# Six of nine chunks multiplied in pairs by one level of Strassen's scheme, with weight sums streamed from DRAM

## The chip, the core and the metric

The kernel runs on one core of a Trainium2 chip. TensorE multiplies, VectorE (DVE), ScalarE (ACT) and GpSimd (POOL) do elementwise work, SyncE (SP) issues DMAs. The metric is device time in microseconds: 858.1 as the median of three runs (858.06 to 858.86). The profile is one further execution, whose span is 856.1 us.

## The reference

Linear attention for 8 batches of 8 heads, 576 tokens of width 64, and an MLP behind it:

```python
q_s = softmax(q, axis=-1); k_s = softmax(k, axis=2)      # both with 1e-9 in the denominator
kv = np.einsum('bhsd,bhse->bhde', k_s, v)
x  = np.einsum('bhsd,bhde->bhse', q_s, kv)               # to 4608 tokens x 512
h  = x @ w_in                                            # 512 -> 2048
g  = h * np.tanh(softplus(h))
out = g @ w_out                                          # 2048 -> 512
```

Everything is fp32. The two products with w_in and w_out are nearly all of the arithmetic.

## The kernel before

**Precision.** TensorE takes operands in a rounded fp32 form (F32R). To keep fp32 accuracy each operand is split into a high part and a low part, the rounded value and what is left, and every product is made of three matmuls: high x high, high x low, low x high. A split costs a rounding copy (the high part) and a subtraction (the low part). The weights come in as 64-bit integers that hold a double; lines 123 to 177 turn them into such pairs on ScalarE, VectorE and GpSimd during the first 115 us.

**Chunks and slots.** Each batch gives a chunk of 512 tokens (its first 512); the 64 remaining tokens of all batches make the ninth chunk, collected through a DRAM tile, `xt_dram`. A chunk has 16 slots, one per block of 128 hidden columns. A slot multiplies first: `h_part` (line 527) adds 4 blocks of 128 input rows x 3 matmuls of 128x512 into one PSUM bank, `ph`. Then Mish on ScalarE (`g_mish`, 553), the high part on VectorE (`g_hi`, 558) and the low part (`g_lo`, 563). Three slots later (`LAG`) `out_mm` (569) adds 4 token blocks x 3 matmuls of 128x512 into four PSUM banks, `po`. So a slot is 12 + 12 matmuls of 128x512, and a chunk 192 + 192.

**Attention items.** 32 items (a batch and two heads each) run beside the MLP: maxima, sums and transposes on VectorE, exponentials on ScalarE (which change its function table, and Mish changes it back), the subtraction of the maximum and the multiplication with the reciprocal on GpSimd (`a_qsub` 270, `a_qmul` 369). Two items make a pair, whose small matmuls `a_pair` (469) places between two blocks; it ends with the split of the chunk's input rows (`x_hi` 509, `x_lo` 514).

**Order.** Everything is scheduled by hand: each engine runs its instructions in the order in which the program issues them. The head of the program is a list of tokens, `FIRST` (line 22): each names a function and its arguments, and a dictionary, `stages`, maps names to functions. It covers the conversion of the weights, the first 8 items and chunk 0 up to its output block 12. From there `group` (601) is a loop: four slots and one attention item per turn, the same for every chunk. DMAs are issued by SP in that same order.

**Memory.** SBUF holds the split weights for the whole run: two tiles `wi` (high and low, 4 x 2048 columns each) and sixteen tiles `wo`. The inputs of two chunks lie in buffers `xa` and `xb`.

Of the kernel before, what the change touches and what calls it, by code (L numbers as in the profile page):

```python
# [43 lines left out]

FILL = dict(
# [8 lines left out]
def attn_mish_mlp(ctx: ExitStack, tc: tile.TileContext, q, v, k2, v2, wu, qs, kt, out):  # L54
# [14 lines left out]
    NSLOT = (B + 1) * NF  # L69
# [10 lines left out]
    sp = ctx.enter_context(tc.tile_pool(name="sp", bufs=4))  # L80
# [11 lines left out]
    turn = []  # L92

    def turn_bank(name):
        turn.append("gh"["gh".index(turn[-1]) ^ 1] if turn else "g")
        return bank(turn[-1], name)


# [7 lines left out]
    wi = [cp.tile([P, HP, DFF], F32R, tag=f"wi{x}", name=f"wi{x}") for x in "hl"]  # L106
# [7 lines left out]

    conv = {}
# [7 lines left out]
    def w_load(j):  # L123
        kind, f = units[j]
        st = xp.tile([P, SM, 2], U32, tag=STAGED.split()[j], name=f"raw_{kind}{f}")
        nc.sync.dma_start(st, wu[f + (NF if kind == "out" else 0)].bitcast(U32).rearrange("p (c z) -> p c z", z=2))
        conv[j] = [st[:, :, 0], st[:, :, 1]]
# [28 lines left out]
    def w_dst(j):  # L156
        kind, f = units[j]
        a = conv[j][2].bitcast(F32)
        if kind == "out" and f not in wo:
            wo[f] = xp.tile([P, 2, DM], F32R, tag=f"wo{f}", name=f"wo{f}")  # L160
        if kind == "in":
            return a.rearrange("p (t c) -> p t c", t=HP), [w[:, :, f * P:(f + 1) * P] for w in wi]
        return a, [wo[f][:, 0], wo[f][:, 1]]
# [20 lines left out]
    xt_dram = dp.tile([B, P, HP, ST], F32, name="xt_dram")  # L184
# [144 lines left out]
    def a_ksub2(f, s):  # L329
        if f >= NITEM:  # L330
            return
        k2, mb = at[f]["k"][:, parts[s]], at[f]["mb"].rearrange("p (h d) -> p h d", h=2)
        sub(nc.vector, k2, k2, mb.unsqueeze(1).to_broadcast(list(k2.shape)))
# [39 lines left out]
    def a_qt(i, b=None):  # L373
# [3 lines left out]
        if i >= COLS:  # L377
            qe = r["qe"].rearrange("p n f -> p (n f)")
            if i % 2:
                qT, qTt = sp.tile([P, SM], F32, tag="wc", name=f"qT{i}"), ap_odd[:, 0]  # L380
# [14 lines left out]
    def a_qt2(i):  # L395
        r = at[i]
        if i in (0, 2, 5, 7):

            t = lp.tile([P, S], F32, tag="kt", name=f"qT{i}") if i < HP else xp.tile([P, S], F32, tag="xb3", name=f"qT{i}")
# [69 lines left out]
    def a_pair(e):  # L469


        f = e + 2
        px = [bank("ef"[j], f"px{e + j}") for j in range(2)] if e >= COLS else None
        if px:
            a_x2(e, px, None, [(0, j, h) for j in range(2) for h in range(2)])
        r = [turn_bank(f"pt{e}_{j}") for j in range(2)]
        pkv = [r[j][:, ST:ST + D + 2] for j in range(2)]
        if px:
            a_x2(e, None, [t[:, 0:ST] for t in r], [(1, j, h) for j in range(2) for h in range(2)])
        if f < NITEM:  # L480
            a_kv2(f, pkv)
        if px:
            for j in range(2):
                x_hi(e + j, at[e + j]["px"])
                x_lo(e + j, at[e + j]["px"])
            for j in range(2):
                a_tail2(e + j)
                a_tail3(e + j)
        if f < NITEM:
            a_kvs2(f)  # L490


# [12 lines left out]
    def a_tail3(i):  # L505
        b, hp = divmod(i, HP)
        nc.sync.dma_start(xt_dram[b, :, hp, :], at[i]["xt"])

    def x_hi(i, src):
        b, hp = divmod(i, HP)  # L510
        xs[i] = xp.tile([P, 2, SM], F32R, tag=f"x{'ab'[b % 2]}{hp}", name=f"xs{i}")
# [4 lines left out]

    tails = {}

    def t_load(t):
        x = tails[t] = pools["wp"].tile([P, SM], F32, tag="w", name=f"xtl{t}")  # L520
        nc.sync.dma_start(x.rearrange("p (b s) -> p b s", b=B), xt_dram[:, :, t, :].rearrange("b p s -> p b s"))

# [4 lines left out]
    def h_part(n, t, b=None):  # L527
        c, f = divmod(n, NF)
        if t == 0:
            gs[n] = bank(b, f"ph{n}") if b else turn_bank(f"ph{n}")  # L530
            fill(f"H{n}", gs[n])
        fs = slice(f * P, (f + 1) * P)
        x = xs[c * HP + t]
        for i, (a, z) in enumerate(((0, 0), (0, 1), (1, 0))):
            nc.tensor.matmul(gs[n], wi[a][:, t, fs], x[:, z], start=t == 0 and i == 0,  # L535
                             stop=t == HP - 1 and i == 2)

    def h_mm(n):
        for t in range(HP):
            h_part(n, t)  # L540

    def open_pools():
        ap.tile([P, 36], F32, tag="gap", name="gap")
        start.__exit__(None, None, None)
        pools["wp"] = ctx.enter_context(tc.tile_pool(name="wp", bufs=4))
        pools["rp"] = ctx.enter_context(tc.tile_pool(name="rp", bufs=LAG + 1))
# [22 lines left out]
    def out_mm(n, parts=range(NC)):  # L569
        c, f = divmod(n, NF)  # L570
        if f == 0:
            for t in range(NC):
# [4 lines left out]
    def out_part(n, t):  # L577
        f = n % NF

        end = NF - 1 - LAG if n // NF == B and t == NC - 1 else NF - 1  # L580
        out_cols(po[t], n, t, slice(0, DM), f == 0, f == end)

    def out_cols(dst, n, t, e, first, last):
        f, g = n % NF, gs[n]
        for i, (a, z) in enumerate(((0, 0), (0, 1), (1, 0))):
            nc.tensor.matmul(dst, g[a][:, t * P:(t + 1) * P], wo[f][:, z, e], start=first and i == 0,  # L586
                             stop=last and i == 2)

    def evac(c, t, copy, cols=slice(0, DM)):
        ob = sp.tile([P, DM], F32, tag="wc", name=f"ob{c}_{t}")[:, cols]  # L590
        copy(ob, po[t])  # L591
        if c < COLS // HP:
            nc.sync.dma_start(out[c * S:c * S + SM, :].rearrange("(p c) e -> p c e", c=NC)[:, t, :], ob)
        elif c < B:
            nc.sync.dma_start(out[c * S + t * P:c * S + (t + 1) * P, :], ob)
        else:
            for j, eng in enumerate((nc.sync, nc.scalar)):
                e = (2 * t + j + 1) * S
                eng.dma_start(out[e - ST:e, cols], ob[j * ST:(j + 1) * ST])

    def group(n):
        i = HP + n // G

        f = i + 1 if i % 2 else i + 2
        pair = i - 1 if i % 2 and COLS < i < NITEM else COLS - 2 if i == COLS else None
        for u in range(G):
            m, o = n + u, n + u - LAG
            if m < NSLOT:
                h_mm(m)
            split = u == 2 and pair is not None  # L610
            if split:
                g_mish(m)
                if pair < COLS:
                    out_mm(o, (0, 1))
                a_pair(pair)
            if u == 0:
                if NITEM <= i < NITEM + HP:
                    t_load(i - NITEM)
                a_qsum(i)
                if i < NITEM:  # L620
                    a_qmul(i)
            if u == 1:
                a_qt(i)
                if i == COLS:
                    a_ksub2(i, 0)
                    a_ksub2(i, 1)
                elif i % 2:
                    a_ksub2(f, 1)
            if 0 <= o < NSLOT:
                out_mm(o, (2, 3) if split and pair < COLS else range(NC))  # L630
            if m < NSLOT and not split:
                g_mish(m)
            if 0 <= o < NSLOT and o % NF == NF - 1:
                for t in range(NC):
                    evac(o // NF, t, nc.scalar.copy if t % 2 else nc.vector.tensor_copy)
            if m < NSLOT:
                g_hi(m)
                g_lo(m)
            if i == COLS and u < 3:
                a_kmx(i + 1 + u)  # L640
                kt_load(i + 3 + u)
            elif i % 2 == 0 and u in (0, 2):
                a_kmx(f + u // 2)
                kt_load(f + u // 2 + 2)
            if u == 1:
                if i == COLS:
                    a_exp2(i, 0)
                    a_exp2(i, 1)
                elif i % 2:
                    a_exp2(f, 1)  # L650
                if pair is not None:

                    nc.scalar.activation(early, ident[:, 0:1], AF.Mish)
                a_qm(i + 1)
            if u == 2:
                if pair is not None:
                    k_load(pair + 4)
                    v_load(pair + 4)
                elif NITEM <= i < NITEM + HP:
                    x_hi(i, tails[i - NITEM])  # L660
                    x_lo(i, tails[i - NITEM])
            if u == 3 and i % 2 == 0:
                a_ksub2(f, 0)
        if i % 2 == 0:
            a_exp2(f, 0)
        a_exp(i + 1)
        q_load(i + 2)
# [15 lines left out]
        G=g_hi, GA=lambda n: g_hi(n, act.copy), GL=g_lo, O=out_mm)  # L683
    with tc.manual_schedule(engines={ET.Activation, ET.PE, ET.DVE, ET.Pool, ET.SP}):
        for token in first:
            name, number, banks = re.fullmatch("([A-Z]+)([0-9]*)([a-h]*)", token).groups()
            stages[name](*([int(number)] if number else []), *([banks] if banks else []))
            if name == "H" and banks in ("g", "h"):
                turn[:] = [banks]
        for n in range(NF, NSLOT, G):  # L690
            group(n)


        end = range(NSLOT - LAG, NSLOT)
        base = sp.tile([P, DM], F32, tag="wc", name="base")
# [68 lines left out]
```

## Time and profile before

| | before |
|---|---|
| median of 3 runs | 858.1 us |
| profiled execution, span | 856.1 us |
| PE busy | 846.2 us (99%) |
| PEld busy | 690.4 us (81%) |
| DVE busy | 433.3 us (51%) |
| ACT busy | 322.8 us (38%) |
| POOL busy | 127.9 us (15%) |
| DMA | 66.39 MB, mean 78 GB/s |

PE is TensorE's matmuls, PEld its weight loads. Matmuls are pipelined and overlap in the records, so that their single durations (about 390 ns) add up to more than the busy time; the pace is read from the starts of blocks. The chain of waits is followed back from the last instruction, at each step to what released it. A row of the windows view gives, for one stretch of the span, the busy microseconds of PE, PEld, DVE, ACT and POOL with their instruction counts, then the granted TensorE clock, the busy share of the 16 DMA engines, and GB/s. A row of the groups view ends with the number of instructions, busy time and mean duration in ns, and the idle time before them with its releaser.

### The profile page before, as it was taken

To read this page: it belongs to the slowest core of one execution; us is meant where nothing else is said; L and a number is where in the kernel's file an instruction comes from. 1 tells how busy PE (TensorE), PEld (TensorE's weight loads), DVE (VectorE), ACT (ScalarE), POOL (GpSimd) and SP (SyncE) were. 2 spreads that over 40 slices of the span, in tenths; PEclk is the share of its full clock that TensorE was granted. 3 is DMA by queue.
4 is the path that set the end of the run, shared out by engine and by line. 5 is a ranking of instruction groups with operands and counts; after the bars stand their busy time and mean duration, and the time that the engine had idled before them with its cause. 6 is when DMAs were issued, how large, how long until landed. Compare 5 with 4: busy or idle time off the path is not lost.

```text
span 856.1 us, 12563 instructions
## 1 busy us (share of the span) xinstructions
PE 846.2 (99%) x4951; PEld 690.4 (81%) x4951; DVE 433.3 (51%) x1111; ACT 322.8 (38%) x498; POOL 127.9 (15%) x111
## 2 busy tenths in 40 slices
PE   8999999999999999999999999999999999999998
PEld 7677778888888888888888888888887888888886
DVE  7998775554645455455545465546543222222221
ACT  6998644424342435243432434243423121111111
POOL 6897110110011111110111110111110000000000
PEclk9999999999999999999999999999999999999999
DMA  9984134212221121212221222121000020001001
GB/s 342 392 322 138 40 115 148 74 42 74 80 72 42 56 85 41 85 29 87 77 81 35 74 91 73 30 74 64 18 14 2 15 75 13 1 1 50 0 1 50
DMA packets 32667, 66.39 MB, mean 78 GB/s; under 512 B 11488, under 2 KB 11744, under 8 KB 32608
## 3 DMA queue, kind: packets, MB, share of 16 engines
q1 hardware_dynamic: 32208, 65.06, 22.9%
q8 instruction: 39, 0.64, 0.3%
q10 hardware_dynamic: 400, 0.52, 0.2%
q14 instruction: 20, 0.16, 0.1%
HBM read 55.09 MB, written 10.49 MB: 77 GB/s over the span
## 4 chain that ended last, share of the span: by engine, by line
PE 90%; DMA 4%; DVE 3%; ACT 1%; issue 1%; SPq 1%; POOL 0%; DVEq 0%
PE po L586 44%; PE ph L535 42%; PE px L414 2%; DMA raw_out<-in_w_dram 2%; DMA v<-in_v_dram 2%; PE pt L451 2%; DMA k<-in_k_dram 1%; DVE wa L148 1%; DVE wc_out L154 1%; DVE k L113 0%; DVE wc_in L154 0%; DVE gl L113 0%; PE po_last L586 0%; PE pt L414 0%; SPq L209 0%
## 5 line engine op out<-in xcount | busy, mean ns | idle before, releaser
L535 PE MATMUL ph<-xs,wih 128*128 128x512 f32 x1152 | 356.4, 391 | 1.3 <-ACT qT L406 1.0
L586 PE MATMUL po<-wo,gh 128*128 128x512 f32 x1146 | 354.8, 391 | 0.0
L535 PEld LDWEIGHTS ph<-xs,wih 128*128 128x128 f32 x1152 | 214.8, 188 | 48.7 <-ACT qT L406 1.4
L586 PEld LDWEIGHTS po<-wo,gh 128*128 128x128 f32 x1146 | 214.0, 188 | 46.0 <-issue 0.8
L555 ACT ACTIVATE y<-ph 128x512 f32<-128x512 f32 x128 | 76.7, 599 | 412.4 <-PE ph L535 345.6
L535 PE MATMUL ph<-xs,wil 128*128 128x512 f32 x576 | 224.3, 389 | 0.0
L586 PE MATMUL po<-wo,gl 128*128 128x512 f32 x573 | 223.1, 389 | 0.0
L560 DVE CAST gh<-y 128x512 fp32r<-128x512 f32 x128 | 54.6, 426 | 266.2 <-ACT y L555 266.1
L535 PEld LDWEIGHTS ph<-xs,wil 128*128 128x128 f32 x576 | 108.1, 188 | 22.6
L586 PEld LDWEIGHTS po<-wo,gl 128*128 128x128 f32 x573 | 107.5, 188 | 22.6
L113 DVE TENSOR_TENSOR gl<-y,gh 128x512 fp32r<-128x512 f32 x128 | 89.4, 699 | 11.9
L371 POOL TENSOR_TENSOR qe<-qe,qs 128x576 f32<-128x576 f32 x24 | 27.9, 1161 | 304.2 <-DVE qs L367 304.2
L113 POOL TENSOR_TENSOR q<-q,qm 128x576 f32<-128x576 f32 (+1 forms) x32 | 38.0, 1192 | 204.9 <-DVE qm L256 194.7
L555 ACT ACT_TABLE_LOAD x24 | 30.8, 1283 | 49.0 <-PE ph L535 48.9
L515 DVE TENSOR_TENSOR xs<-px,xs 128x512 fp32r<-128x512 f32 x32 | 20.6, 686 | 42.9 <-ACT xs L512 42.9
L339 ACT ACT_TABLE_LOAD x23 | 29.5, 1283 | 5.5 <-DVE k L113 5.1
L357 DVE TENSOR_REDUCE qs<-qe 128x18 f32<-128x576 f32 x24 | 18.1, 752 | 25.8 <-ACT qe L346 25.8
L265 DVE TENSOR_REDUCE qm<-q 128x18 f32<-128x576 f32 (+1 forms) x32 | 24.4, 763 | 9.2 <-DMA q<-in_q_dram 4.7
L591 DVE COPY ob<-po 128x512 f32<-128x512 f32 x16 | 11.0, 691 | 26.1 <-PE po L586 26.1
L237 DVE TENSOR_REDUCE mxd<-kt 128x1 f32<-128x576 f32 x32 | 23.8, 745 | 0.5 <-DMA kt<-in_kt_dram 0.5
L246 DVE STREAM_TRANSPOSE mb<-mxd 32x32 f32<-32x32 f32 x96 | 19.4, 202 | 1.8
L113 POOL TENSOR_TENSOR wil<-wc_in,wih 128x512 fp32r<-128x512 f32 x15 | 19.4, 1305 | 5.6 <-ACT wih L167 5.2
(113 smaller groups left out, 563.0 us busy)
## 6 DMA issues: line engine op xcount, KB each, us to landing
kt<-in_kt_dram SPq DMA_DIRECT2D x32, 288.0 KB, 3.0
v<-in_v_dram SPq DMA_DIRECT2D x14, 594.0 KB, 5.5
raw_in<-in_w_dram SPq DMA_DIRECT2D x16, 512.0 KB, 7.7
raw_out<-in_w_dram SPq DMA_DIRECT2D x16, 512.0 KB, 6.7
out_dram<-ob SPq DMA_DIRECT2D x32, 256.0 KB, 2.2
k<-in_k_dram SPq DMA_DIRECT2D x14, 576.0 KB, 4.1
q<-in_qs_dram SPq DMA_DIRECT2D x24, 288.0 KB, 2.8
q<-in_q_dram SPq DMA_DIRECT2D x8, 320.0 KB, 6.2
```

Source lines behind the costliest of these rows:

```text
L113: eng.tensor_tensor(out, a, b, ALU.subtract)
L237: nc.vector.tensor_reduce(mxd, r["kt"], axis=AX.X, op=ALU.max, negate=i < HP)
L246: nc.vector.transpose(mb[o:o + 32, h], mxd[h].to_broadcast([32, 32]))
L265: nc.vector.tensor_reduce(qm, qt, axis=AX.X, op=ALU.max)
L339: nc.scalar.activation(k2, k2, AF.Exp)
L357: nc.vector.tensor_reduce(z, q2, axis=AX.X, op=ALU.add)
L371: eng.tensor_tensor(q2, q2, z.unsqueeze(2).to_broadcast(list(q2.shape)), ALU.mult)
L515: nc.vector.tensor_tensor(xs[i][:, 1], src, xs[i][:, 0].bitcast(F32), ALU.subtract)
L535: nc.tensor.matmul(gs[n], wi[a][:, t, fs], x[:, z], start=t == 0 and i == 0, stop=t == HP - 1 and i == 2)
L555: nc.scalar.activation(y, gs[n], AF.Mish)
L560: copy(hi, gs[n])
L586: nc.tensor.matmul(dst, g[a][:, t * P:(t + 1) * P], wo[f][:, z, e], start=first and i == 0, stop=last and i == 2)
```

## The change

The first three chunks stay as they were. The last six (five batches and the chunk of remaining tokens) are taken in three pairs, k = 0 to 2, and both products of a pair are done by one level of Strassen's scheme in Winograd's form. For the first product the weights are cut in two along the hidden columns and along the 512 input rows (blocks A11, A12, A21, A22) and the inputs along the input rows and along the tokens (B11 ... B22; a token half holds 256 tokens of each of the two chunks). Seven block products take the place of eight:

```
S1 = A21+A22  S2 = S1-A11  S3 = A11-A21  S4 = A12-S2       (weights)
T1 = B12-B11  T2 = B22-T1  T3 = B22-B12  T4 = B21-T2       (inputs)
P1 = A11 B11  P2 = A12 B21  P3 = S4 B22  P4 = A22 T4
P5 = S1 T1    P6 = S2 T2    P7 = S3 T3
C11 = P1+P2   C12 = P1+P6+P5+P3   C21 = P1+P6+P7+P4   C22 = P1+P6+P5+P7
```

(T4, and so P4, is held with its sign such that it adds.) The second product does the same with the Mish values as B and w_out as A, and gives the output transposed, in a second output tensor that the host transposes back.

- **Weight sums.** During chunks 1 and 2, for each of 16 units (8 of w_in, 8 of w_out): GpSimd adds high and low part back together (`w_whole`, 2 additions of 128x512) and forms the four sums (`w_mix`, 4 of 128x256); ScalarE rounds (`w_mix_hi`, 128x1024), VectorE subtracts (`w_mix_lo`, 128x1024), SP stores to a DRAM tile `ws` (`w_keep`, 3 DMAs of the unmixed blocks; `w_mix_out`, 8 DMAs). Together 112 block operands of 256 KB, in the order in which TensorE wants them.
- **Weight stream.** GpSimd fetches two operands at a time (512 KB) into a ring of six SBUF tiles (`w_fetch`), 56 per pair, in the order of the tokens `F0` to `F171`. A fetch waits until TensorE is done with the tile that it overwrites. The tiles are former weight and input buffers.
- **Inputs.** `x_raw` copies the attention result to SBUF unsplit; VectorE forms the four sums (`x_mix`, 128x1024), then each of seven operands is split (`x_mix_hi` on ScalarE, `x_mix_lo` on VectorE, 128x1024).
- **First product.** 8 blocks n x 7 products x 6 matmuls of 128x512. P1, P6, P5, P3 add into one PSUM bank, P7 and P4 into another, P2 into a third. Between them ScalarE copies the partial sum out (`partial`, 24 per pair) and VectorE adds the other bank (`joined`, 24 per pair), and Mish runs on the result (`g_mish_quad`, 32 per pair).
- **Second product.** The Mish values are mixed (`g_mix`, 16 of 128x1024 per pair, alternately VectorE and GpSimd) and split (`g_mix_hi` on ScalarE and `g_mix_lo` on VectorE, 28 each, 128x1024, in a ring of four tiles). Again 56 x 6 matmuls of 128x512. 6 partial copies, 8 joins, 8 stores of 256 KB per pair.
- **Order.** `FIRST` is as before. In place of the loop `group` stands a second list of tokens, `LATER`, for all engines and the whole rest. The attention items run on through chunks 1 and 2 and pair 0, the last ones at the start of pair 1; the items of pair k+1 come during pair k.

```diff
+LATER = """
+WW0 WM0 WK0 HM16g WK1 MK9 WH0 WK2 OP13.0 WK4 WL0 OP13.1 LK11 OP13.2 WK6 YM16 U8.0v OP13.3 WP0 G16 HM17h GL16 U8.1v Q8
...
+GX1.0.1v XR28 A1.3.2 F72 C1.3.0 A1.2.5 J1.3.0 N1.3.0 A1.3.7 C1.2.3 F73 GH1.1.1 J1.2.3 A1.3.6 N1.2.3 GK1.1.1 PK28df
...
+A2.2.7 C2.1.3 J2.1.3 A2.2.6 F126 N2.1.3 A2.1.3 C2.2.2 A2.1.4 N2.1.1 F127 GX2.0.0p A2.3.1 J2.1.2 N2.1.2 A2.3.2 C2.3.0
...
-    wi = [cp.tile([P, HP, DFF], F32R, tag=f"wi{x}", name=f"wi{x}") for x in "hl"]
+    wi = [cp.tile([P, 2, HP, P], F32R, tag=f"w{f}", name=f"wi{f}") for f in range(NF)]
...
+    NW = 14 * NH
+    ws = dp.tile([NW // 2, P, 2, 2 * 2 * P], F32, name="ws")
...
+    def w_whole(j, eng="p"):
...
+            engines[eng].tensor_tensor(a[:, i], w[:, 0].bitcast(F32), w[:, 1].bitcast(F32), ALU.add)
...
+    def x_mix(k, o, eng="v"):
+        b11, b12, b21, b22 = (x_quad(k, kh, th) for kh in range(2) for th in range(2))
+        d, a, b = ((b11, b12, b11), (b12, b22, b12), (b22, b22, b11), (b21, b21, b22))[o]
+        sub(engines[eng], d, a, b)
...
+    RING = ["w0", "w1", "xa0", "xa1", "xa2", "xa3"]
...
+    def w_fetch(e):
+        t = ring[e] = (cp if RING[e % 6][0] == "w" else xp).tile(
+            [P, 2, 2, 2, P], F32R, tag=RING[e % 6], name=f"ws{e}")
+        nc.gpsimd.dma_start(t.rearrange("p s z j c -> p s (z j c)"), ws[e % (NW // 2)].bitcast(F32R))
...
+    def first_product(k, n, p):
+        t = k * NW + place[1, p, n]
+        w = ring[t // 2][:, t % 2]
+        if p in (1, 2, 7):
+            letter = {1: "gac"[n % 3], 2: "h", 7: "eb"[n % 2]}[p]
+            psb[p, k, n] = bank(letter, f"{ {1: 'px', 2: 'pz', 7: 'py'}[p] }{k}_{n}")
+        dst = psb[{6: 1, 5: 1, 3: 1, 4: 7}.get(p, p), k, n]
+        for j in range(2):
+            for i, (a, z) in enumerate(halves3):
+                nc.tensor.matmul(dst, w[:, a, j], xc[k, p][z][:, j].rearrange("p b s -> p (b s)"),
+                                 start=p in (1, 2, 7) and j == 0 and i == 0, stop=j == 1 and i == 2,
+                                 skip_group_check=p not in (1, 2, 7))
...
+    def partial(k, n, q):
+        nc.scalar.copy(g_quad(k, n)[q], psb[1, k, n])
+
+    def joined(k, n, q):
+        g = g_quad(k, n)[q]
+        nc.vector.tensor_tensor(g, psb[2 if q == 0 else 7, k, n], g, ALU.add)
...
+    def g_mix_hi(k, p, h):
+        t = split[k, p, h] = pools["sc"].tile([P, 2, 2, SM], F32R, tag=f"s{ring_at[p, h] % 4}", name=f"gs{k}_{p}_{h}")
+        nc.scalar.copy(t[:, 0], gq[k, h][G_PART[p]])
+
+    def g_mix_lo(k, p, h):
+        t = split[k, p, h]
+        sub(nc.vector, t[:, 1], gq[k, h][G_PART[p]], t[:, 0].bitcast(F32))
...
-        for n in range(NF, NSLOT, G):
-            group(n)
...
+        for token in first + LATER.split():
+            name, numbers, letters = re.fullmatch("([A-Z]+)([0-9.]*)([a-z]*)", token).groups()
+            stages[name](*(int(x) for x in numbers.split(".") if x), *([letters] if letters else []))
```

In `LATER`, `A` and `BB` are the block products of the two stages (pair, block, product), `C` and `J` partial and join, `N` Mish, `GX`, `GH`, `GK` mix, high and low part of the Mish values, `XA`, `XH`, `XL` the same for the inputs, `DP`, `DJ`, `DS` partial, join and store of the output, `F` a fetch; `WW`, `WM`, `WH`, `WL`, `WK`, `WP` make the weight sums; `HM`, `YM`, `G`, `GL`, `OP` are a slot of an old chunk; the others are attention.

More of the change, by code (lines that the diff above doesn't have):

```diff
@@ L68, in attn_mish_mlp @@
     NG = NF // G
-    NSLOT = (B + 1) * NF
+    NPL = 3
+    NSLOT = NPL * NF
+    NSC = (B + 1 - NPL) // 2
+    NH = NF // 2
     NITEM = B * HP
@@ L571, in out_mm @@
         if f == 0:
-            for t in range(NC):
+            for t in parts:
                 po[t] = bank("abcd"[t], f"po{c}_{t}")
@@ L601, in group @@
[L601 to L667, printed above, removed]
@@ new lines, in second_product @@
+    def second_product(k, f, p):
+        t = k * NW + place[2, p, f]
+        if p == 4 and place[2, p, f] < 7:
+            t += NW
+        w = ring[t // 2][:, t % 2]
+        key = {6: 1, 5: 1, 3: 2, 4: 7}.get(p, p)
+        if p in (1, 2, 7) and (key, k) not in psb:
+            psb[key, k] = [bank(c, f"{ {1: 'qx', 2: 'qz', 7: 'qy'}[p] }{k}_{m}")
+                             for m, c in enumerate({1: "hg", 2: "ae", 7: "cb"}[p])]
+        first = p in (1, 2, 7, 3) and f == 0
+        g = split[k, p, f // 2]
+        for m in range(2):
+            for i, (a, z) in enumerate(halves3):
+                nc.tensor.matmul(psb[key, k][m], w[:, a, m], g[:, z, f % 2], start=first and i == 0,
+                                 stop=f == NH - 1 and i == 2, skip_group_check=p in (4, 5, 6))
```

369 lines of the change are left out of this document (284 added, 85 removed).

## The prediction

> **What bounds the kernel now.** I read the page's totals first, then the chain that ended last.
>
> ```profile
> span 856.1 us, 12563 instructions
> ...
> PE 846.2 (99%) x4951; PEld 690.4 (81%) x4951; DVE 433.3 (51%) x1111; ACT 322.8 (38%) x498; POOL 127.9 (15%) x111
> ...
> PE 90%; DMA 4%; DVE 3%; ACT 1%; issue 1%; SPq 1%; POOL 0%; DVEq 0%
> ```
>
> TensorE is busy for 99% of the span and carries 90% of the chain, so the question is its pace. The chain in order of time gives it; the last two rows are the same view of the final stretch.
>
> ```profile
> 115.02 2.73 PE po L586 x12
> 117.75 2.77 PE ph L535 x12
> 120.52 2.72 PE po L586 x12
> ...
> 294.59 2.95 PE po L586 x12
> ...
> 340.53 2.95 PE po L586 x12
> ...
> 849.90 2.16 PE po_last L586 x18
> ...
> 852.14 0.43 DVE ob L707
> ```
>
> A block of 12 matmuls (128x512) takes 2.72 us in both products, so one costs 0.2267 us. From 294.59 to 340.53 are 45.94 us: 16 blocks (43.52) and one attention pair on TensorE, which so costs 2.42. As a check: chunk 1's first hidden block starts at 117.75 (the x12 before it is the thirteenth output block of chunk 0). 3456 matmuls less 192 and 156 already done leave 3108, or 704.5 us; twelve pairs add 29.0; that ends at 851.3, and the last matmul of the trace ends at 852.06. After 117.75 TensorE therefore never waits. The windows, by stage, show what stands beside it (PE, PEld, DVE, ACT, POOL busy; clock; DMA share; GB/s):
>
> ```profile
> 22.00:44.00 22.00, 20.23 (x101) 15.34 (x102) 20.50 (x34) 20.96 (x41) 19.80 (x15) 1.00 1.02 392
> 44.00:66.00 22.00, 22.00 (x166) 17.57 (x164) 20.32 (x42) 20.68 (x35) 21.18 (x17) 1.00 0.84 310
> 66.00:88.00 22.00, 20.86 (x96) 16.01 (x95) 19.36 (x32) 17.17 (x34) 13.90 (x11) 1.00 0.40 126
> ...
> 271.00:317.00 46.00, 46.00 (x282) 37.66 (x281) 24.21 (x71) 16.78 (x24) 4.64 (x4) 1.00 0.18 54
> ...
> 690.00:740.00 50.00, 50.00 (x222) 41.42 (x221) 11.96 (x21) 6.41 (x11) 0.00 (x0) 1.00 0.05 11
> ```
>
> In the steady stage VectorE stands at 53% and ScalarE at 36%; only before 88 us, where the weights are converted, are they at 80 to 95%, and only there does TensorE lose time: 1.77, 0 and 1.14 us, 2.91 of 66, or 4.4%.
>
> **What is removed.** Two chunks by the old way take 2x(192+192) = 768 matmuls. By the new way each product is 8 blocks x 7 products x 6 matmuls = 336, together 672. Three pairs save 288 matmuls of the same shape, and at 0.2267 that is 65.3 us, all on the chain. Attention and the first 117.75 us keep their work. At the end the last store grows from 64 to 256 KB behind an addition over 512 columns in place of 256:
>
> ```profile
> L515 DVE TENSOR_TENSOR xs<-px,xs 128x512 fp32r<-128x512 f32 x32 | 20.6, 686 | 42.9 <-ACT xs L512 42.9
> ...
> out_dram<-ob SPq DMA_DIRECT2D x32, 256.0 KB, 2.2
> ...
> out_dram<-ob SPq DMA_DIRECT2D x2, 64.0 KB, 2.1
> ```
>
> 0.69 - 0.43 and 2.2 - 2.1 make +0.4. So the floor is 856.1 - 65.3 + 0.4 = 791.2 in the profiled execution. The median of the runs is 858.1, 2.0 above its span, so the floor of the time is 793.
>
> **What is added on the other engines.** These rows price it.
>
> ```profile
> L113 DVE TENSOR_TENSOR gl<-y,gh 128x512 fp32r<-128x512 f32 x128 | 89.4, 699 | 11.9
> L555 ACT ACTIVATE y<-ph 128x512 f32<-128x512 f32 x128 | 76.7, 599 | 412.4 <-PE ph L535 345.6 <-issue 66.5
> L560 DVE CAST gh<-y 128x512 fp32r<-128x512 f32 x128 | 54.6, 426 | 266.2 <-ACT y L555 266.1
> ...
> L371 POOL TENSOR_TENSOR qe<-qe,qs 128x576 f32<-128x576 f32 x24 | 27.9, 1161 | 304.2 <-DVE qs L367 304.2
> ...
> L113 POOL TENSOR_TENSOR wil<-wc_in,wih 128x512 fp32r<-128x512 f32 x15 | 19.4, 1305 | 5.6 <-ACT wih L167 5.2
> ...
> L591 ACT COPY ob<-po 128x512 f32<-128x512 f32 x19 | 11.2, 589 | 17.8 <-PE po L586 17.8
> ...
> L113 DVE TENSOR_TENSOR k<-k,pb 128x1152 f32<-128x1152 f32 x2 | 2.7, 1347 | 0.0
> ...
> L349 ACT ACTIVATE k<-k 128x1152 f32<-128x1152 f32 x2 | 2.3, 1150 | 0.0
> ```
>
> The new 128x1024 operations have no row; scaled from 1152 columns they cost 1.20 us on VectorE (twice 0.699 is the upper end) and 1.02 on ScalarE, and scaled from 576 columns 2.06 on GpSimd (twice 1.305 is the upper end). An attention item follows from 271 to 317 us, which holds two items and eight slots: VectorE 24.21 - 8x1.125 - 2x0.686 leaves 6.9 each, ScalarE (16.78 - 8x0.599)/2 = 6.0 with its table loads, GpSimd 2.3. Counting the new order's tokens, I divide it by TensorE's work.
>
> Stretch one, chunks 1 and 2: TensorE 792 matmuls and 6.5 pairs, 195 us, with 13 items where the old kernel had about 8. VectorE: 32 slots 36, items 90, the weight sums' low parts 13x1.20 = 16, the first pair's inputs 10x1.20 = 12, evacuations 3, together 156 us, 80%. ScalarE 121 (62%), GpSimd 103 (28 sums at 1.305, 56 half-width ones at 0.65, items 30), 53%. Stretch two, the first product of pair 0: TensorE 82; VectorE 6 items 41, 22 joins at 0.686, 11 wide operations and two evacuations, 71 (87%); ScalarE 36 for items, 23 copies, 27 Mish, 6 wide copies, 73 (89%). Stretch three, its second product: TensorE 79; VectorE 24 low parts, 5 differences, 11 for the next pair, all at 1.20, 3 items and 8 joins, 74 (94%); ScalarE 72%. From there the items run out: VectorE 50, 68, 32 and 53% in the last four stretches (81, 76, 76 and 80 us of TensorE).
>
> So no engine's sum passes TensorE's, but two stretches run at the load where the old kernel lost 4.4%. I put 4.4% on their 161 us, 7 us, and 1 us on the first stretch (80%, between the 53% that lost nothing and the 88% and above that lost): 8 us of waits, with 0 and the worst window's 8% of all 356 us, 28, as bounds. What is late there is a PSUM bank or a split operand: in the first product TensorE may add to a bank only once ScalarE has copied the partial sum out, and the shortest such gap in the order is two products of 1.36 us, while ScalarE's queue is in order and holds table loads. On VectorE a late join keeps GpSimd's next attention operation waiting, and behind that stands the next weight fetch.
>
> Collisions raise these loads:
>
> ```profile
> L113 DVE TENSOR_TENSOR gl<-y,gh x128: 691/693/1466, 121.9 to 842.3; 128x512 fp32r<-128x512 f32 x128
> ```
>
> One VectorE subtraction took 1466 ns where the median is 693: something can hold an operation for 0.77 us. The Trainium skill ("SBUF — State Buffer", section "SBUF: two separate sides") says why: VectorE with two SBUF inputs and a GpSimd operation that reads SBUF exclude each other for a whole instruction. By that rule stretch three, with GpSimd computing for 17 of 79 us and 40 such VectorE operations, would wait 40 x 0.22 x 1 us = 9 us, and its VectorE sum of 83 would pass TensorE's 79 by 4; the sum above has 3.5 for this stretch, so the rule changes little.
>
> **The weight stream.** From pair 0 on every two products need one fetch of 512 KB issued by GpSimd: 168 used, one per 2.72 us, 193 GB/s. The trace has no DMA from GpSimd. The nearest rows are those of SP, issues in order of time, then times to landing.
>
> ```profile
> 22.20 0.33 SPq L126 DMA_DIRECT2D raw_out<-in_w_dram  x1
> ...
> 28.60 0.33 SPq L126 DMA_DIRECT2D raw_in<-in_w_dram  x1
> ...
> raw_in<-in_w_dram SPq DMA_DIRECT2D x16, 512.0 KB, 7.7
> ...
> k<-in_k_dram SPq DMA_DIRECT2D x14, 576.0 KB, 4.1
> ```
>
> Six requests of 512 KB, the same 4 KB per partition, went out in 22.20 to 28.60, 1.28 us apart, at the window's 392 GB/s. If GpSimd's requests overlap likewise, the stream uses half of that and hides behind TensorE: six ring slots are 16 us of matmuls, a landing 4.1 to 7.7. If only one is in flight, each costs at least 4.1. I take 1.28, since the engines and the shape are those of that row, and cost it at nothing; the cover is gone above 2.72 us per fetch. GpSimd's own time then is 56x1.28 and 17 us of differences per pair, 89 of 152. The 29 MB of weight sums go out through SP beside attention's loads, 16 units x 11 requests x 0.33 = 58 us of issue over 195 us and 150 GB/s. Queued behind a weight store that waits for VectorE are the loads of the next item, landing in some 4 us and needed an item (15 us) later: hidden.
>
> **Forecast and rivals.** Forecast: 793 + 8 = 801, from 796 to 808; chance 0.45.
> Rival one, the order fits and TensorE never waits: 793, 790 to 796; chance 0.2. For it, the old order lost nothing at 53%; against it, 94%.
> Rival two, the busy stretches lose like the worst window, 8% of 356 us, or a late join passes through GpSimd's queue to the fetches: 793 + 28 = 821, 808 to 835; chance 0.23. For it, three queues in order feed each other; against it, 44 to 66 us, where 92 to 96% cost nothing.
> Rival three, on the other side: GpSimd's requests do not overlap and TensorE waits for every fetch. It decides from 2.72 us; the saving is gone at 2.72 + 65.3/168 = 3.11 us. At 4.1 us, 168 x 1.38 = 232, so 1025. For it, no row shows this queue; against it, SP's spacing. Chance 0.12, of it 0.02 between 835 and 856. The Trainium skill ("DMA: Bandwidth & Descriptors", section "Anatomy of one DMA — SWDGE (gpsimd) path") prices one such DMA alone at about 2.0 us and bytes/436e3, an estimated 3.2 us here, which one at a time would make 874; no row of this trace bears on it.
>
> About 0.2%, 1.7 us, is what can be told from no change. Faster takes the first three cases and the 0.02: 0.9; the same 0.01; slower 0.09. The range runs from 790 (floor less 3 for the first 117 us) to 830, leaving out rival three and the end of rival two.
>
> **What would show it.** Right: about 288 fewer 128x512 matmuls; twelve matmuls still in 2.72 us; TensorE idle gaps gathered in stretches two and three, released by ScalarE copies, joins or low parts; none in pairs 1 and 2; fetches landing well inside 13 us. Wrong: gaps of equal size at every second product released by a DMA (rival three), TensorE busy throughout (rival one), or gaps in pairs 1 and 2 as well, where no engine is above 70%.

## The result and the profile after

The changed kernel takes 865.5 us (863.7 to 866.7) against 858.1 (858.06 to 858.86) before: 1.0085 times as long, interval 1.0070 to 1.0099. It is slower by 7 us; 801 was forecast.

The page's totals and its clock row, after:

```profile
span 863.3 us, 12978 instructions
...
PE 810.2 (94%) x4654; PEld 644.1 (75%) x4654; DVE 625.6 (72%) x1136; ACT 474.2 (55%) x676; POOL 397.1 (46%) x403
...
PEclk9999997879998999989899999999999999999999
...
PE 38%; DVE 34%; DMA 11%; issue 4%; SPq 4%; POOL 4%; ACT 4%; DVEq 0%; POOLq 0%; ACTq 0%
```

TensorE runs about 300 records fewer, as intended, but it no longer carries the chain: its share there fell from 90% to 38%. And the clock row has slices below 9. The windows show where (PE, PEld, DVE, ACT, POOL busy; clock; DMA share; GB/s): chunks 1 and 2 in three rows, the two products of pair 0, a stretch of pair 2's first product.

```profile
118.00:150.00 32.00, 25.83 (x167) 19.96 (x166) 17.91 (x49) 16.47 (x18) 12.22 (x13) 0.85 0.98 324
150.00:200.00 50.00, 37.22 (x210) 27.97 (x209) 31.95 (x77) 17.54 (x22) 19.72 (x17) 0.82 0.74 240
...
118.00:357.00 239.00, 210.25 (x1393) 163.50 (x1392) 192.92 (x438) 124.95 (x152) 124.58 (x114) 0.93 0.61 195
...
357.00:456.00 99.00, 89.93 (x594) 69.55 (x592) 82.51 (x193) 64.95 (x96) 49.97 (x54) 0.93 0.83 264
456.00:540.00 84.00, 81.05 (x424) 65.31 (x425) 78.02 (x118) 45.60 (x58) 38.26 (x38) 0.98 0.73 230
...
702.00:778.00 76.00, 76.00 (x337) 62.96 (x336) 24.12 (x30) 33.73 (x55) 21.97 (x31) 1.00 0.69 201
```

From 118 to 150 us the DMA engines are full and *every* compute engine is idle for a good part. From 702 to 778 TensorE never stops: that part came out as forecast.

The table gives each stage from its first matmul to the next stage's, in us, beside TensorE's own work by the prediction. Its last two rows are for everything after 117.75: TensorE's idle time, and time at half clock (in e8 the dummy matmuls count as work).

| | work | after | e1 | e2 | e4 | e8 | e9 | e10 |
|---|---|---|---|---|---|---|---|---|
| chunks 1, 2 | 195 | 239.0 | 222.6 | 205.7 | 198.3 | 219.4 | 218.9 | 224.4 |
| pair 0, first product | 82 | 99.3 | 98.9 | 90.7 | 87.1 | 99.0 | 99.3 | 90.3 |
| pair 0, second | 79 | 84.2 | 85.4 | 86.3 | 84.2 | 83.6 | 84.2 | 86.2 |
| pair 1, first | 81 | 81.4 | 80.7 | 80.7 | 81.4 | 81.4 | 81.4 | 80.7 |
| pair 1, second | 76 | 80.7 | 82.5 | 79.4 | 83.4 | 78.8 | 79.6 | 79.4 |
| pair 2, both | 156 | 157.3 | 157.3 | 157.3 | 157.3 | 157.4 | 157.4 | 157.3 |
| TensorE idle | | 44.3 | 31.8 | 18.5 | 10.3 | 21.1 | 29.6 | 29.5 |
| at half clock | | 51.2 | 41.0 | 6.8 | 10.2 | 17.1 | 30.7 | 23.9 |

After is 73 us over the work; chunks 1 and 2 hold 44 of them and pair 0's first product 17. So the 65 us saved did arrive, and a larger sum was lost elsewhere. TensorE's idle time and half of its time at half clock make 70 of the 73.

TensorE's first loss is a gap of 4.57 us at 138 us. Two rows of the waits of chunks 1 and 2, after (who waits, for whom, us in total, times, longest):

```profile
PE po L660 <- DVE ob L667: 13.2, 4, 6.0
DVE qT L493 <- POOL qe L480: 9.8, 1, 9.8
```

In that gap TensorE waits for VectorE's copy of an output block; VectorE had waited 9.8 us for a multiplication of GpSimd; and GpSimd had stood still for 15.9 us, from 121.0 to 136.9, until the sums of the first unit were stored (its row is shown at e9). SP issued those eight stores from 129.39 on, behind 15 stores of unmixed blocks.

The longest waits of the next stretch, 150 to 180 us:

```profile
ACT L455 <- DVE odd L494: 17.7, 1, 17.7
POOL q L215 <- DVE qm L365: 17.6, 1, 17.6
DVE qm L374 <- DMA q<-in_qs_dram: 14.7, 1, 14.7
ACT w_in L733 <- POOL m_in L728: 7.6, 1, 7.6
PEld px L523 <- DVE qT L493: 7.3, 1, 7.3
PE px L523 <- DVE qT L493: 6.5, 1, 6.5
```

These end in one thing: VectorE waits 14.7 us for a load of queries, and GpSimd, ScalarE and TensorE wait for VectorE. What SP did before it issued that load (start, duration, instructions in a row):

```profile
117.95 8.66 SPq L696 DMA_DIRECT2D ws<-wi  x12
...
136.61 6.59 SPq L696 DMA_DIRECT2D ws<-wo  x9
143.24 2.26 SPq L696 DMA_DIRECT2D ws<-wi  x3
145.55 6.89 SPq L696 DMA_DIRECT2D ws<-wo  x9
152.55 0.65 SPq L308 DMA_DIRECT2D k<-in_k_dram  x1
...
157.98 0.84 SPq L326 DMA_DIRECT2D q<-in_qs_dram  x1
```

These are stores of unmixed weight blocks (`w_keep`, tokens `WK`), 0.72 us each and one after the other, and the load stands behind them.

### The profile page after: what moved, and what is told of

Same layout as the page of the kernel before. It is cut to its first block, busy times and chain, and to the rows that moved or that the text cites. A ratio compares the mean times of both kernels' runs of the same rounds, so it can differ in the third digit from the quotient of the medians.

```text
span 863.3 us, 12978 instructions
## 1 busy us (share of the span) xinstructions
PE 810.2 (94%) x4654; PEld 644.1 (75%) x4654; DVE 625.6 (72%) x1136; ACT 474.2 (55%) x676; POOL 397.1 (46%) x403
## 4 chain that ended last, share of the span: by engine, by line
PE 38%; DVE 34%; DMA 11%; issue 4%; SPq 4%; POOL 4%; ACT 4%; DVEq 0%; POOLq 0%; ACTq 0%
PE px L808 10%; DVE gs L215 6%; PE qx L825 6%; PE py L808 5%; DVE sw L364 4%; PE qz L825 3%; SPq L696 3%; DVE xl L215 3%; PE pz L808 3%; PE qy L825 3%; PE ph L617 3%; DMA q<-in_qs_dram 3%; PE po L660 3%; DVE g L215 2%; POOL m_in L728 2%
## 5 line engine op out<-in xcount | busy, mean ns | idle before, releaser
L791 POOL DMA_DIRECT2D ws<-ws x172 | 93.5, 544 | 232.9 <-PE px L808 60.6
L215 DVE TENSOR_TENSOR gs<-g,gs 128x1024 fp32r<-128x1024 f32 x84 | 115.6, 1385 | 40.1 <-ACT gs L858 40.1
L660 PE MATMUL po<-wo,gh 128*128 128x512 f32 x384 | 126.8, 412 | 13.2 <-DVE ob L667 13.2
L808 PE MATMUL px<-xh,ws 128*128 128x512 f32 x384 | 132.6, 394 | 6.1 <-ACT g L836 6.1
L858 ACT CAST gs<-g 128x1024 fp32r<-128x1024 f32 x84 | 87.7, 1051 | 73.2 <-PE qx L825 30.4
L825 PE MATMUL qx<-gs,ws 128*128 128x512 f32 x432 | 101.7, 391 | 2.3 <-DVE gs L215 2.2
L660 PEld LDWEIGHTS po<-wo,gh 128*128 128x128 f32 x384 | 73.9, 197 | 37.3 <-DVE ob L667 15.5
L617 PE MATMUL ph<-xs,wi 128*128 128x512 f32 x384 | 95.7, 395 | 1.7 <-ACT qT L515 1.3
L825 PEld LDWEIGHTS qx<-gs,ws 128*128 128x128 f32 x432 | 80.7, 188 | 20.8 <-DVE gs L215 3.9
L660 PE MATMUL po<-wo,gl 128*128 128x512 f32 x192 | 77.9, 406 | 0.0
```

Source lines behind the costliest of these rows:

```text
L215: eng.tensor_tensor(out, a, b, ALU.subtract)
L617: nc.tensor.matmul(gs[n], wi[f][:, a, t], x[:, z], start=t == 0 and i == 0, stop=t == HP - 1 and i == 2)
L660: nc.tensor.matmul(po[t], g[a][:, t * P:(t + 1) * P], wo[f][:, z], start=f == 0 and i == 0, stop=f == NF - 1 and i == 2)
L791: nc.gpsimd.dma_start(t.rearrange("p s z j c -> p s (z j c)"), ws[e % (NW // 2)].bitcast(F32R))
L808: nc.tensor.matmul(dst, w[:, a, j], xc[k, p][z][:, j].rearrange("p b s -> p (b s)"), start=p in (1, 2, 7) and j == 0 and i == 0, stop=j == ...
L825: nc.tensor.matmul(psb[key, k][m], w[:, a, m], g[:, z, f % 2], start=first and i == 0, stop=f == NH - 1 and i == 2, skip_group_check=p in ...
```

## The experiments

The results of e1, e6, e7, e8 and e11 rest on several runs and carry intervals; the others are one run each. The kernel before took 857.9 beside all of them. The table's stages come from one profiled execution of each; that of e1 took 850.8 us, the longest of its four.

### e1: the unmixed blocks' stores spread

```diff
+later = [t for t in LATER.split() if t[:2] != "WK"]
+for s, j in enumerate((0, 13, 1, 2, 3, 4, 5, 6, 7, 14, 15, 8, 9, 10, 11, 12)):
+    i = next(i for i, t in enumerate(later) if t[:4] == f"HM{16 + 2 * s}")
+    later.insert(i + 1, f"WK{j}")
```

> The 48 stores of unmixed weight blocks, which SP issues in a row from 118 to 163 us, are spread instead: three after every second hidden block of chunks 1 and 2. Theory A (stores ahead of attention's loads on SP's queue and on the DMA engines make VectorE wait, and TensorE's idle time then halves its clock): the 22 us of TensorE gaps and most of the half clock between 118 and 200 us go, so 830 to 845 us. Theory B (GpSimd's weight sums hold VectorE through the port that they share): the stores were beside the path, 858 to 866 us.

Measured: 846.5 us, 0.9856 of before (0.9833 to 0.9879), 19 us less than the change; theory A had said 830 to 845. The second load of queries now goes out at 136.67 in place of 157.98, GpSimd's wait for the first unit's stores falls from 15.9 to 3.3 us, and the first window of chunk 1 reads

```profile
118.00:150.00 32.00, 31.51 (x208) 25.34 (x210) 28.34 (x72) 20.24 (x22) 15.62 (x17) 1.00 0.67 225
```

against 25.83 of TensorE and 17.91 of VectorE above. Same work, same bytes, same queue; only the order of 48 stores is another. This version already beats the kernel before.

### e2, e3, e4: without the stores, without the sums, without both

```diff
 e2, e4
+later = [t for t in LATER.split() if t[:2] not in ("WK", "WP")]
-nc.gpsimd.dma_start(..., ws[e % (NW // 2)].bitcast(F32R))
+nc.gpsimd.dma_start(..., v2[e % 14]...)
 e3, e4
-            engines[eng].tensor_tensor(a[:, i], ..., ALU.add)      # w_whole
-            engines[eng].tensor_tensor(m[:, o], x, y, op)         # w_mix
```

> All stores of weight blocks and weight sums are left out, and the fetches read 4 KB per partition of the attention values' input instead, so the output is not the reference's. All arithmetic and all fetches stay. Theory A: chunks 1 and 2 fall from 239 us to about 200, the whole to 815 to 825 us. Theory B: they keep their length within 10 us, 853 to 865 us.

> GpSimd's 96 additions for the weight sums are left out; ScalarE's rounding and VectorE's low part read the plain weights in their place, and all stores and fetches stay, so the output is not the reference's. Theory A: the loads still wait behind the stores, 855 to 865 us. Theory B: VectorE's slowed operations (low part 978 ns, high part 644, small copies 311) go back to about 700, 430 and 170, which takes some 40 us out of VectorE's sum in chunks 1 and 2; the whole falls to 815 to 830 us.

> Both left out, the stores and GpSimd's additions for the weight sums; the output is not the reference's. Both theories: what is left is the order and the pairs themselves, 795 to 805 us. If it stays above 815, a third cause sits in the order of chunks 1 and 2 or in the first product of pair 0.

Measured: 823.3, 846.0 and 815.1 us. e2 is what theory A said; e3 lies between the two theories, and e4 at the value that was to mean a third cause. No fetch in after waits for a store, so it isn't the fetches' other source that gains here. So the stores cost 42 us of 865.5 (31 where the sums are out), GpSimd's 96 additions 19.5 (8 where the stores are out), both together 50. The two overlap by 11, probably because an engine that is late for one is late for the other anyway. How the additions act is seen on VectorE. Groups with mean duration, of after and then of e3:

```profile
L215 DVE TENSOR_TENSOR gl<-y,gh 128x512 fp32r<-128x512 f32 x32 | 31.3, 978 | 1.5
L364 DVE COPY sw<-qm 32x18 f32<-32x18 f32 x96 | 29.8, 311 | 1.8
L640 DVE CAST gh<-y 128x512 fp32r<-128x512 f32 x32 | 20.6, 644 | 0.0
```

```profile
L215 DVE TENSOR_TENSOR gl<-y,gh 128x512 fp32r<-128x512 f32 x32 | 24.1, 752 | 1.5
L364 DVE COPY sw<-qm 32x18 f32<-32x18 f32 x96 | 20.5, 214 | 1.8
L640 DVE CAST gh<-y 128x512 fp32r<-128x512 f32 x32 | 15.8, 494 | 4.0 <-ACT y L635 3.9
```

The same operations on the same tiles take 30 to 45% longer while GpSimd adds. Over chunks 1 and 2 that is 192.92 us of VectorE above against, in e3 and in e4,

```profile
118.00:341.00 223.00, 203.82 (x1398) 160.05 (x1397) 167.95 (x454) 126.96 (x155) 42.55 (x33) 0.96 0.68 219
```

```profile
118.00:316.00 198.00, 197.54 (x1391) 157.11 (x1390) 166.19 (x452) 125.58 (x154) 42.08 (x33) 1.00 0.36 112
```

In after VectorE is busy 25 us longer than in e3, in 16 instructions fewer, and GpSimd 82 us longer. e3 takes out both; what each is worth by itself was not separated. With stores and additions out TensorE is busy for 197.5 of 198 us there, at full clock.

### e5: all the stores, an eighth of their bytes

```diff
-        nc.sync.dma_start(dst if z is None else dst[:, z], src)
+        if z is None:
+            dst, src = dst[:, :, 0:32], src[:, :, 0:32]
+        else:
+            dst, src = dst[:, z, 0:32], src[:, 0:32]
+        nc.sync.dma_start(dst, src)
```

> The changed kernel with all its 176 weight stores issued at the same places with the same number of rows, but each row cut to 32 of 256 columns, an eighth of the bytes; the fetches read the attention values' input, so the output is not the reference's. If the loads wait for SP, which issues the stores one by one (0.72 us each at the start of chunk 1), the time stays near the changed kernel's, 850 to 866 us. If they wait for the bytes on the DMA engines (98% busy from 118 to 150 us), it comes down to what leaving the stores out gave, 820 to 830 us.

Measured: 849.4 us. Of the stores' 42 us, 16 went with seven eighths of the bytes and 26 stayed. The 48 stores of unmixed blocks were issued in 0.47 us each (median) instead of 0.72. The rows of 128 bytes still occupied the DMA engines for 0.53 of the first window, so the bytes cost at least 16, and at most 26 stay with the 176 requests themselves: their place in SP's order and the buffers that they hold. Neither theory alone is right.

### e6: the unmixed stores from ScalarE's queue

```diff
 on e1
-    def w_put(key, z, src):
+    def w_put(key, z, src, eng=nc.sync):
...
-                w_put((1, p, f), None, wi[u][...])
+                w_put((1, p, f), None, wi[u][...], nc.scalar)
```

> The spread stores of unmixed blocks, issued by ScalarE instead of SP. If SP's order is what is left of the stores' cost after spreading (846.5 us against 823.3 without stores), the attention loads come earlier: 830 to 840 us. If it is the bytes, or if ScalarE's queue pays with the same 0.7 us per store, 843 to 852 us.

Measured: 851.5 us, 0.9941 (0.9913 to 0.9969): worse than e1 by 5. The 48 requests take 0.39 us of ScalarE's queue each (median), some 19 us; that these are the 5 us is likely and was not separated. The stores of sums stayed where they were.

### e7: GpSimd's share of the Mish mixing given to VectorE

```diff
 on e1
+later = [re.sub("p$", "v", t) if re.match("GX[12]", t) else t for t in later]
```

> The spread stores, and in pairs 1 and 2 all differences of the Mish values on VectorE, none on GpSimd. Theory B for the pairs (GpSimd's 2.6 us differences hold VectorE's low parts through the shared port, up to 3.4 us in place of 1.22): the second product of pair 1, 82.5 us with the spread stores and 76 by its matmuls, falls to 77 to 79 and the whole to 840 to 844 us. If VectorE's own longer sum costs as much, 845 to 850 us.

Measured: 847.9 us, 0.9888 (0.9859 to 0.9918), which can't be told from e1. Pair 1's second product took 84.1 us against 82.5; 77 to 79 was expected. So moving GpSimd's 2.8 us mixing operations gains nothing in pairs 1 and 2; whether they cost time where they are stays open, since VectorE then carries them.

### e8: TensorE kept busy over three gaps

```diff
 on e1
+    def keep_busy(n, letter):
+        t = bank(letter, f"busy_{letter}")
+        for _ in range(n):
+            nc.tensor.matmul(t[:, 0:P], ident, ident, start=True, stop=True)
...
+for at_token, letter, n in (("PK8ef", "h", 10), ("PK10ef", "g", 18), ("OP32.0", "e", 22)):
+    later.insert(later.index(at_token), f"FB{n}{letter}")
```

> The spread stores, and dummy matmuls (128x128, some 2, 3.5 and 4.4 us) ahead of the three longest waits of TensorE in chunks 1 and 2 (for VectorE's split of the inputs of items 8 to 11 and its evacuation of chunk 1). If the half clock after such a wait is an answer to the idle time, about 17 us of half clock go with the gaps, and the whole falls by 5 to 9 us, to 838 to 842. If the half clock has another cause, nothing is gained and the dummies cost up to 5 us: 846 to 852.

Why this was asked: rows of TensorE in the changed kernel around one gap (start, duration, operation, idle before it).

```profile
142.71 1.22 PE L660 MATMUL po<-wo,gh 128*128 128x512 f32 x2 [4.57 <-DVE ob L667]
...
144.16 1.05 PE L660 MATMUL po<-wo,gh 128*128 128x512 f32 x2
...
153.08 0.62 PE L660 MATMUL po<-wo,gh 128*128 128x512 f32 x2
```

Two matmuls take 0.62 us together at 153 us, but 1.05 to 1.22 after a gap of 4.57 us, and the granted clock of that stretch is one half:

```profile
142.70:150.00 7.30, 5.68 (x12) 3.71 (x13) 6.12 (x13) 4.58 (x7) 3.56 (x4) 0.50 1.03 340
```

The Trainium skill ("TensorE: Matmul & The Clock Gate", section "HAM oscillation — how this bites in real kernels") has a rule for this: an idle gap over some 3.4 us drops the array to half rate. The gap of 4.57 us agrees, but in the same trace shorter ones are followed by half clock as well: 1.83 us at 362.4, 3.02 at 382.3, 2.05 at 418.0 and 2.10 at 493.4, each for 3.4 to 6.8 us, while 1.82 us at 340.4 is not. A gap well under 3.4 us can be enough here.

Measured: 842.4 us, 0.9816 (0.9799 to 0.9832), 4 us less than e1 and just above the expected 838 to 842. In the two profiled executions (842.8 and 850.8 us) time at half clock fell from 41.0 to 17.1 us. But only chunks 1 and 2 hold dummies: there it fell from 20.5 to 6.8 us, and the stage from 222.6 to 219.4. So the half clock does answer to the idle time, and its removal gave 3 us where half of 13.7 would be 7. That TensorE is behind another engine there anyway is a likely reason and was not tested. The other stages differ between the two executions without a change of theirs. This is the fastest of the complete versions, 1.8% below the kernel before.

### e9, e10: which of the stores

```diff
 e9
+later = [t for t in LATER.split() if t[:2] != "WK"]
 e10
+later = [t for t in LATER.split() if t[:2] != "WP"]
```

> The changed kernel without the 48 stores of unmixed blocks (WK); the 128 stores of sums (WP) stay; the ring is filled from the attention values' input (what is left out: the weights of the pairs, so their values). Theory A (what costs is the row of stores at the start of chunk 1, 43 of the 48 within 45 us, with attention's loads behind them in SP's queue): the gain is that of spreading them, 19 us, or more: 840 to 847. Theory B (what costs is the sums' stores, which wait in SP's queue for VectorE and ScalarE): nearly the whole 42 us stay, 857 to 865.

> The changed kernel without the 128 stores of sums (WP); the 48 stores of unmixed blocks stay as in the changed kernel; ring filled as in the run before (left out: the weights of the pairs). Theory A: 844 to 865, since the row at the start stays. Theory B: 823 to 832, near the run without any store (823.3).

Measured: 843.9 and 841.5 us. Neither theory alone: the 48 unmixed stores cost 21.6, the 128 stores of sums 24.0, 45.6 together against 42.2 for both at once. They act in different ways. In e10, with the unmixed stores alone, the DMA engines are as full in the first window as in the changed kernel, but TensorE stands still for 0.6 us of it, not 6.2:

```profile
118.00:150.00 32.00, 31.37 (x205) 25.54 (x204) 21.51 (x51) 16.83 (x19) 13.99 (x14) 1.00 1.01 338
```

So full DMA engines alone don't stop TensorE there. What the row of stores does is to hold up the load of queries, which goes out at 153.60. VectorE waits 17.0 us for it and TensorE 10.4 us for VectorE, its longest wait of the stage:

```profile
DVE qm L374 <- DMA q<-in_qs_dram: 17.0, 1, 17.0
...
PE px L523 <- DVE qT L493: 10.4, 1, 10.4
```

In e9, with the sums' stores alone, the first window is undisturbed (DMA share 0.53, TensorE busy for 31.5 of 32 us), and the time is lost over the whole of chunks 1 and 2 and in pair 0's first product, 99.3 us as in the changed kernel; in e10 that product took 90.3. (The additions and stores of the last units run on into this product, in after until 412 us.) What these stores hold up is shown by the waits of chunks 1 and 2 in after:

```profile
POOL w_in L718 <- DMA ws<-w_in: 23.0, 4, 15.9
...
POOL w_out L718 <- DMA ws<-w_out: 15.1, 4, 12.0
```

There is one buffer for a unit's sums; GpSimd can't start the next unit before the last one is stored, and its attention operations stand behind that in its queue. In after the two kinds meet: the first unit's stores are issued behind 15 unmixed ones, and the 15.9 us are GpSimd's wait for them.

### e11: the loads ahead of the sums' stores

```diff
 on e8
+for t in [t for t in later if t[:2] in ("LK", "LQ")]:
+    i = later.index(t)
+    w = [x for x in range(max(0, i - 30), i) if later[x][:2] == "WP"]
+    if w:
+        later.insert(w[0], later.pop(i))
```

> The version with stores spread and dummy matmuls (842.4), and each load of keys or queries that stood up to 30 tokens behind the stores of a unit's sums (WP) now stands in front of them, 20 loads. If loads queued behind stores that wait for VectorE and ScalarE are what is left of the stores' cost in chunks 1 and 2, that stage falls from 219 us to 205 to 212 and the time to 830 to 838. If the sums themselves (GpSimd against VectorE) are what is left, the stage stays at 217 to 220 and the time at 840 to 844. Worse than 844 would say that the loads now wait for their buffers and hold the stores up.

Measured: 879.2 us, 1.0262 of before (1.0234 to 1.0289); chunks 1 and 2 took 254.0 us. The third case came, at 37 us over e8. SP's own waits from 118 to 260 us, of e8 and then of e11:

```profile
SPq L696 <- ACT w_in L733: 17.3, 7, 6.0
...
SPq L326 <- ACT qe L455: 5.2, 5, 2.7
...
SPq L318 <- DVE mxd L346: 2.7, 2, 1.9
```

```profile
SPq L318 <- DVE mxd L346: 21.9, 4, 8.1
SPq L696 <- ACT w_in L733: 21.1, 4, 7.1
...
SPq L326 <- ACT qe L455: 13.8, 6, 8.1
```

In front, the loads of keys (L318) and queries (L326) wait for their own buffers, and the stores wait behind them; GpSimd then waits for the stores and ScalarE for GpSimd (in e11 `ACT w_in` waits 42.4 us for GpSimd from 118 to 260). So it isn't that one kind stands on the wrong side of the other: one queue in order ties two cycles of buffers together, and each can stop the other. A second buffer for the sums might loosen that tie; it was not tried.

## Why the prediction was wrong

**Right.** The floor: pair 1's first product and both of pair 2 run within 1.4 us of TensorE's work, at 12 matmuls in 2.72 us. The weight stream is hidden, more easily than priced:

```profile
L791 POOL DMA_DIRECT2D ws<-ws x172: 527/530/753, 253.0 to 850.5; - x172
...
DMA to landing us min/median/max: 3.4/4.3/7.8
```

0.53 us of GpSimd a fetch, not 1.28, and no wait of TensorE for a fetch. Rival three fell, though its side, slower, is the one that came. The Trainium skill ("DMA: Bandwidth & Descriptors", section "Anatomy of one DMA — SWDGE (gpsimd) path") gives an estimated 3.2 us for one such DMA, below the 4.3 measured beside other traffic. The fetches follow each other faster than they land, one per 2.72 us, so they overlap and neither figure sets the time. Of the busy stretches two and three, the products of pair 0, the sums came near where stores and additions are out. The windows of e4:

```profile
315.00:402.00 87.00, 85.09 (x529) 66.45 (x531) 70.60 (x172) 62.93 (x94) 37.40 (x41) 0.98 0.76 240
402.00:486.00 84.00, 81.24 (x499) 65.38 (x496) 78.05 (x123) 46.95 (x59) 38.43 (x39) 0.98 0.74 229
```

VectorE is busy for 70.6 and 78.1 us, where 71 and 74 were forecast. The stages take 5.1 and 5.2 us more than TensorE's work, 10 where 7 were priced. The wait named, a PSUM bank behind ScalarE's partial copy, is there too; from 118 us on in after:

```profile
PE px L808 <- ACT g L836: 6.1, 3, 3.0
```

**The step that failed** is the paragraph on the weight stores: "Queued behind a weight store that waits for VectorE are the loads of the next item, landing in some 4 us and needed an item (15 us) later: hidden." Four things in it were wrong.

- The cost was spread evenly over 195 us (58 us of issue, 150 GB/s), while the order of the tokens puts all 48 unmixed stores into the first 45 us. In the first 32 us the DMA engines are full (0.98, 324 GB/s).
- A request was priced at 0.33 us and took 0.72 in that row. The six requests that the prediction shows were themselves 1.28 us apart, at a DMA share of 1.02: 0.33 us is the length of one, not the pace of many.
- The margin of 15 us was held against the landing alone, not against what stands ahead in the queue: the load of queries went out 21 us later than it does in e1. The list of tokens would have told it: the diff shows `WK0 WK1 WK2 WK4 WK6` within its first line.
- The buffer that a store releases was not followed to its next writer, GpSimd, which waited up to 15.9 us for it, with attention's operations behind.

Together these cost 42 us, priced at nothing. The signs that were named looked for TensorE's gaps in stretches two and three; 44 of the 73 us lie in stretch one, which was given 1. The whole miss is 64 us: 14 stay in e4, the additions bring it to e2's 823.3 (8), and the stores to 865.5 (42).

**Mis-sized, not missed:** the first stretch's waits, 1 us. Its VectorE sum of 156 us became 193: 166 in e4, without additions and stores, where the 10 more were not looked into, and 25 from e3 to after by collisions with GpSimd, which were priced for the third stretch only, where no additions of weights run. Of VectorE's operations only those with two SBUF inputs were counted; the copies and casts, with one, were held as well (311 against 214, 644 against 494). The Trainium skill ("SBUF — State Buffer", section "SBUF: two separate sides") does name a second class beside them, VectorE's 2-port modes; that the casts ran in such a mode is not shown by any run here. (A hint is that the same cast takes 422 ns from SBUF and 681 from PSUM, medians of after.) Without the stores the additions cost 8 us, with them 19.5.

**Missed:** the clock. The sum had TensorE's waits at their own length, though a gap of some us slows what follows. 51 us at half clock are at most 26 us of time; of this e8 shows 3 to 4 by experiment, with 13.7 us of half clock taken away.

Rival two had the form of what came, "three queues in order feed each other", but had a late join pass through GpSimd's queue to the fetches. What came through GpSimd's queue was a wait for a store, and it reached attention and VectorE. Rival two was priced by a share of the old kernel's waits, and that kernel stored no weights through SP. The range missed for the same reason: its ends came from these waits and from the fetch, none from the stores.

**Left open:** e4 stands 14 us above the forecast with neither stores nor additions. 7 of its 22 us over the floor lie in pair 1's second product, in which VectorE, the busiest engine beside TensorE, stands at 71%. A gap of 3.9 us behind a partial copy, 7 us after its start, and 3.4 us at half clock after that make 5.6 of the 7. The rest was not taken apart. How the 24 us of the sums' stores divide between the buffer and SP's order was not separated either; e11 shows only that they hang together.

## What to carry to other kernels

Cost a DMA by what stands ahead of it in its issuing queue, at the place in the order where it stands, and not by an average over the stage; then follow the buffer that it reads to the next writer. A stage that adds stores to a queue of loads needs the stores spread between the loads: the same 48 stores cost 19 us more in a row than spread. More buffers are another way that no run here tried. And where TensorE's idle gaps reach some us, look at the clock row before the waits are added up.

## What was not expected of the hardware

- The time that SP needs to issue a store depends on how much the DMA engines have to move. Stores of 256 KB, minimum, median and maximum in ns, in after and in e1:

```profile
L696 SPq DMA_DIRECT2D ws<-wi x24: 433/712/1289, 118.0 to 156.0; - x24
```

```profile
L696 SPq DMA_DIRECT2D ws<-wi x24: 424/478/1660, 118.1 to 222.7; - x24
```

The stores are the same. In e5, where they stand in the same row with an eighth of the bytes, the median is 467 ns: it is the bytes, not the row. 256 KB in 0.72 us are 364 GB/s, near the 324 GB/s that the window moved, so with the engines full issuing seems to run at the pace of the transfers.

- Small copies on VectorE pay as much for GpSimd as large operations. Minimum, median and maximum, in before and in after:

```profile
L255 DVE COPY sw<-qm x96: 163/168/173, 112.9 to 636.1; 32x18 f32<-32x18 f32 x96
L560 DVE CAST gh<-y x128: 362/427/578, 121.2 to 841.8; 128x512 fp32r<-128x512 f32 x128
```

```profile
L364 DVE COPY sw<-qm x96: 163/171/1245, 112.7 to 553.3; 32x18 f32<-32x18 f32 x96
L640 DVE CAST gh<-y x32: 361/422/1516, 124.0 to 357.2; 128x512 fp32r<-128x512 f32 x32
```

The longest is 1.07 us over the median for 32x18 elements and 1.09 for 128x512. Where the time goes can be read from the ends. In after, 24 of these copies, 17 of these casts and 18 of the subtractions `gl` began while an elementwise operation of GpSimd ran, and none ended before it. The twelve longest of each ended 27 to 35 ns (copies), 281 to 289 ns (casts) and 546 to 554 ns (subtractions) after that operation's end. So an operation of these three kinds that begins under one of GpSimd's is finished only when that one is over, however small it is.
